# Second unit's state sums and half of its first outputs ahead of the first up-projections, in other banks

## The chip, the cores and the metric

The kernel runs on one core of one Trainium2 chip. The metric is the device time of one execution in microseconds (us), less is better; beside it stands the span of a profiled execution, from the first instruction of the program to the last. The engines are called as in the profile: PE (TensorE, matrix multiplications; PEld is its loading of weights), DVE (VectorE), ACT (ScalarE), POOL (GpSimd) and SP (SyncE, which issues most DMAs).

## The reference

A state-space scan in chunks over x (4 batches, 8 heads, 768 positions, 32 channels; states of 16), then a feed-forward block with a squared ReLU over the 3072 rows of 256 values that the scan gives:

```python
for c in range(nc):                        # chunks along the sequence
    cum = np.cumsum(log(a) of the chunk, axis=-1)
    L = np.exp(cum[:, :, :, None] - cum[:, :, None, :]) * causal
    M = np.einsum('bhin,bhjn->bhij', Cc, Bc) * L
    y_intra = np.einsum('bhij,bhjd->bhid', M, xc)
    y_inter = np.einsum('bhin,bhnd->bhid', Cc, state) * np.exp(cum)[..., None]
    y[:, :, sl] = y_intra + y_inter
    state = exp(sum of log(a)) * state + sum_j(decay_from_j * B_j x_j)
x = y.transpose(0, 2, 1, 3).reshape(B * S, H * D)
h = np.maximum(x @ w_in, 0.0)              # w_in: 256 x 2048
out = h * h @ w_out                        # w_out: 2048 x 256
```

## The kernel before

The work is cut into 12 units of 256 positions of one batch: units 0 to 3 are the first third of each batch, 4 to 7 the second, 8 to 11 the last. A unit is also a block of 256 rows of the feed-forward part, and the blocks are called a to l, so that unit 0 is block a and unit 1 is block b. Within a unit there are two halves of 128 positions with a state carried from one to the next.

For one of the first four units the steps are these, each a word of the list `ORDER` (lines 48 to 70), with the number of the unit behind it:

- `ldB`, `ldC`, `ldx` load B, C and x; `pb` and `pc` write B and the scaled C into `jt` (lines 169 to 188), `px` writes the scaled x into `xs` (line 190).
- `tr` turns `jt` round on PE (line 213), into two banks; `tc` copies that to `bct` in SBUF (DVE or ACT).
- `mt` computes the scores into the banks 0 to 3, 16 matmuls (line 243). `mk` is a mask multiplication on DVE straight out of a bank (line 252); `sc` copies a bank to SBUF on ACT (line 257), and `ms` masks that copy (line 261). Each `mk` or `sc` takes the next of the four banks, in the order 0, 1, 2, 3.
- `u` makes the state sums from `xs` and `jt`, 16 small matmuls (line 299); `us` copies them to SBUF (ACT, lines 349 and 352); `sf` makes from them the state `Sd` that the second half needs (DVE, line 396).
- `ina` and `inb` make the first outputs, each with two of the four masked score tiles and 16 matmuls (line 320); `ca` adds what the carried state gives (line 284).
- `t` copies the finished outputs into `T` (ACT or DVE, line 338), the input of the feed-forward part.

`p2` sums the second table of decays on PE (lines 529 to 642), and `pd` copies it to SBUF on ACT (lines 648 and 649). `id` are matmuls on constants whose result nobody reads (line 562).

The feed-forward part of a block has eight steps. Up-projection: `a0` is block a, step 0, four matmuls (line 475) into one bank, then a ReLU on ACT out of that bank (line 482); `qa0` squares it on DVE (line 488). Down-projection: `A0`, four matmuls (line 503), summed over the eight steps in bank 7 (bank 6 for block b). For the first four steps of block a the up-projection is in two parts: `al0` to `al3` make the two matmuls on the first half of the 256 inputs, `ah0` to `ah3` the two on the second half, and then the ReLU. The weights of `w_in` come in four DMAs that POOL issues, `wi0` to `wi3` (`wi0` and `wi1` hold the two halves of the inputs for the steps 0 to 3, `wi2` the steps 4 and 5, `wi3` the steps 6 and 7), those of `w_out` in `wo0` to `wo3`.

Every engine executes its own instructions in the order in which the list names them; between engines there are semaphores, set where one instruction writes what another reads, or writes over what another still reads. PSUM has eight banks of 512 columns. The list can name a bank (`al0@0`; `tr2@23` names two; `u1:57:6` puts the outputs of unit 1 into the banks 5 and 7 and the state sums of its first half into 6). Where it doesn't, a rotating list hands one out:

```python
turn = list(range(6))
def bank():
    h = want.pop(0) if want else next(h for h in turn if h not in busy)
    if h in turn:
        turn.remove(h)
        turn.append(h)
    return h
```

`busy` holds the banks that are taken in the order of the list: `mt` takes 0 to 3, and each `mk` or `sc` gives one back; `tr` takes two until its copies. A bank that an up-projection takes by itself is not held in `busy`; that its reader is done is seen to by the semaphores. For `u` without banks, the neighbouring free pair that stands earliest in `turn` is taken and moved to the end; the pair of `u3:45` is named and does not move anything in `turn`. At the word `bk`, in the third block, the list is set to 4, 5, 6.

Of the kernel before, what the change touches and what calls it, by code (L numbers as in the profile page):

```python
# [30 lines left out]
def kernel(  # L31
# [17 lines left out]
        fa1:a jz0:v ef jz1:p id3:512 ti fa0:s la0:s id4:512 pi eb ldB0:s ac0:v ldC0:a sk0 ku sp la1:a pbh0:p hd  # L49
        id1:256 pc0:v pbl0:v mb:a id1:384 trC0 ps iv:8:16 tcC0:1:a tcC0:0:v trB0 la2:s tcB0:2:v pk id1:512 iv1:0:8  # L50
        id1:512 ldx0:s mt0 hold wi0 la3:s px0:v ldC1:s su id2:512 ldB1:s wi1 ldx1:s u0:67 mk0 fq mk0 gC2:v mk0 ac1:v pc1:p sc0
        pb1:a jz2:a id2:512 tr1 id3:512 tc1:1:a tc1:0:v to ms0:p sf0 sk1 wo0 wi2 px1:p mt1 ina0 inb0 ca0 pp1:a mk1 mk1 t0:aa
        sc1 us0 mk1 fr p2@4 pd al0@0 al1@1 ldC2:s al2@5 al3@7 u1::6 ina1 ms1:v wo1 wi3 pc2 inb1 sf1 ca1 t1:va ah0 us1 ah1 qa0 ah2
        ldB2:s qa1 ah3 wo2 b0@2 qa2 qa3 qb0 b1@3 qb1 b2@4 b3@5 A0 A1 pb2:p tr2 B0 B1 zb0 qb3 gB3:v ldx2:s ldB3:s ldC3:s ldx3:s b4 a4
        iv:32:64 zb1 tc2:1:v tc2:0:v b5 sb1 sb0 qb4 a5 qb2 qa4 mt2 sc2 B3 iv:16:32 px2 pc3 wo3 px3 mk2 mk2 sc2 A3
        A2 ms2:v ms2:v qa5 a6 b6 pb3:a B2 a7 qb5 b7 u2 ina2 inb2 sf2 ld4 A4 tr3 ca2 tc3:1:v t2:aa B4 us2 B5
        tc3:0:v qa6 u3:45 pc4 mt3 A5 us3 sc3 c5 qb7 qb6 mk3 za3 pb4 ldC5:s ldB5:s c3 qa7 c4 qc5 c0 qc3 px4 tr4 ldx5:s pb5
        pc5 sa3 c1 c6 ldC6:s tr5 ldB6:s ldx6:s qc4 qc0 A6 px5 pq A7 wm c2 B6 c7 C0 ms3:v mk3 qc6 mk3 qc7 afC2 pc6 B7
# [838 lines left out]
```

## Time and profile before

| | |
|---|---|
| time, median of 3 runs | 114.05 us (113.71 to 114.88) |
| the profiled execution: time | 114.34 us |
| the profiled execution: span | 112.6 us |
| PE busy | 107.0 us (95%) |
| DVE, ACT, POOL busy | 82.2 us (73%), 76.9 us (68%), 49.5 us (44%) |
| granted TensorE clock | 1.000 |

A line of the timeline gives the start and the duration in us, the engine, the line of the kernel, the operation, what is written and read, how many instructions are drawn together, and in brackets the idle time of the engine before it and what ended that. The ends of matmuls are modelled, so that the matmuls of one group overlap those of the next by up to some 0.2 us. A line of the table of stretches gives for each engine the busy time and the number of instructions, and then the granted clock, the DMA share and the rate.

### The profile page before, as it was taken

The page shows a single profiled execution, that of the slowest core. Times are in us where ns is not written, and L with a number is a line of the kernel's source. Part 1 is how long each engine was busy: PE and PEld are TensorE (multiplying, and loading weights), DVE is VectorE, ACT ScalarE, POOL GpSimd, SP SyncE. Part 2 cuts the span into 40 slices and gives each one's busy share as a digit, 9 for nine tenths or more (in the row PEclk, how much of TensorE's full clock was granted, in tenths as well). Part 3 has the DMA queues.
Part 4 walks back from the last instruction along what each step waited for, and adds up shares of the span by engine and source line. Part 5 has one row for each costly group of instructions (what it writes and reads, how often), then busy time and mean ns, then how long its engine had stood idle before and what let it go on. Part 6 is the DMA issues. An engine that isn't in the chain of part 4 may idle for free.

```text
span 112.6 us, 3683 instructions
## 1 busy us (share of the span) xinstructions
PE 107.0 (95%) x1451; PEld 92.1 (82%) x1452; DVE 82.2 (73%) x190; ACT 76.9 (68%) x159; POOL 49.5 (44%) x96
## 2 busy tenths in 40 slices
PE   6988699999999999999999999999999999999990
PEld 2435589897998989989979989889899899899980
DVE  1689558996993898979966999779489298355440
ACT  1557487976894785685687686777876867866840
POOL 7579651488476574286074883283340020000000
PEclk9999999999999999999999999999999999999999
DMA  1999999499889899997897867799940020020203
GB/s 35 200 188 175 206 204 221 82 206 183 127 173 116 101 278 69 101 183 85 108 168 107 188 99 75 161 135 108 182 122 0 6 96 0 23 76 0 93 0 93
DMA packets 67025, 13.44 MB, mean 119 GB/s; under 512 B 63104, under 2 KB 65472, under 8 KB 67008
## 3 DMA queue, kind: packets, MB, share of 16 engines
q1 hardware_dynamic: 64320, 10.88, 63.2%
q0 software_dynamic: 1408, 2.10, 10.8%
q10 hardware_dynamic: 1280, 0.23, 1.1%
q8 instruction: 11, 0.18, 0.7%
q14 instruction: 6, 0.05, 0.2%
HBM read 10.58 MB, written 3.15 MB: 122 GB/s over the span
## 4 chain that ended last, share of the span: by engine, by line
PE 88%; DMA 3%; SPq 3%; ACT 2%; issue 1%; DVE 0%; ACTq 0%
PE pp L459 76%; PE pp L268 7%; DMA B_nat<-in_B_dram 3%; PE pp L237 2%; PE pp L243 2%; SPq L664 1%; SPq L138 1%; PE pp L213 1%; PE pp L562 1%; ACT T L226 1%; ACT sc L257 0%; DVE Sd L396 0%; ACT jt L183 0%; SPq L121 0%; ACT osl L855 0%
## 5 line engine op out<-in xcount | busy, mean ns | idle before, releaser
L482 ACT ACTIVATE hb<-pp 128x512 bf16<-128x512 f32 x96 | 54.5, 605 | 21.0 <-PE pp L459 19.5
L459 PE MATMUL pp<-T,w_in_b 128*128 128x256 bf16 x384 | 53.5, 273 | 0.8 <-ACT P_sb L649 0.8
L459 PE MATMUL pp<-w_out_b,h 128*128 128x256 bf16 (+1 forms) x400 | 53.9, 268 | 0.0
L488 DVE TENSOR_TENSOR h<-hb 128x512 bf16<-128x512 bf16 x96 | 44.0, 474 | 13.0 <-ACT hb L482 12.3
L459 PEld LDWEIGHTS <-w_in_b 128*128 128x128 bf16 x384 | 41.4, 114 | 2.9 <-issue 1.1
L459 PEld LDWEIGHTS <-h 128*128 128x128 bf16 x400 | 37.6, 98 | 4.5 <-issue 1.0
L252 DVE TENSOR_TENSOR mts<-pp,mask 128x512 bf16<-128x512 f32 x43 | 28.5, 677 | 0.8 <-PE pp L237 0.8
L195 POOL TENSOR_TENSOR xs<-x_nat,Pinv 128x256 bf16<-128x256 f32 (+1 forms) x19 | 14.0, 750 | 11.7 <-DMA x_nat<-in_x_dram 8.7
L384 POOL TENSOR_TENSOR Sd<-z,Pquad 128x256 bf16<-128x256 f32 x16 | 10.7, 679 | 12.3 <-DVE z L368 7.3
L175 POOL TENSOR_TENSOR jt<-C_nat,P_sb 128x128 bf16<-128x128 f32 x22 | 9.7, 460 | 9.1 <-DMA C_nat<-in_C_dram 7.3
L368 DVE SCALAR_TENSOR_TENSOR z<-z,Ptot,us 128x64 f32<-128x64 f32 x8 | 3.0, 372 | 6.8 <-ACT us L352 4.8
L562 PE MATMUL pp<-const-bfloat16-1.0 128*128 128x512 bf16 (+2 forms) x17 | 6.3, 491 | 1.0 <-PEq L881 0.8
L183 POOL CAST jt<-B_nat 128x256 bf16<-128x256 f32 x9 | 4.3, 476 | 6.6 <-DMA B_nat<-in_B_dram 4.5
L510 ACT COPY osb<-pp 128x512 f32<-128x512 f32 x11 | 6.4, 583 | 0.4 <-PE pp L459 0.4
L268 PE MATMUL pp<-mts,xs 64*32 64x128 bf16 (+1 forms) x288 | 5.4, 219 | 0.0
L268 PE MATMUL pp<-bct,Sd 128*128 128x128 bf16 x40 | 4.2, 220 | 0.2 <-DVE Sd L396 0.2
L268 PEld LDWEIGHTS <-xs 64*32 64x32 bf16 (+1 forms) x288 | 3.6, 93 | 0.4 <-issue 0.2
L562 PEld LDWEIGHTS <-const-bfloat16-1.0 128*128 128x128 bf16 x18 | 1.6, 114 | 2.5 <-issue 2.2
L268 PEld LDWEIGHTS <-Sd 128*128 128x128 bf16 x40 | 3.0, 98 | 0.7 <-DVE Sd L396 0.4
L226 ACT CAST T<-pp 128x256 bf16<-128x256 f32 x5 | 1.8, 373 | 2.6 <-PE pp L268 2.4
L268 PEld LDWEIGHTS <-jt 64*32 64x32 bf16 (+1 forms) x128 | 1.6, 90 | 1.9 <-issue 0.8
L257 ACT CAST sc<-pp 128x512 bf16<-128x512 f32 x5 | 2.9, 608 | 0.3 <-PE pp L243 0.2
(80 smaller groups left out, 59.5 us busy)
## 6 DMA issues: line engine op xcount, KB each, us to landing
out_dram<-osb SPq DMA_DIRECT2D x11, 256.0 KB, 2.9
x_nat<-in_x_dram SPq DMA_DIRECT2D x6, 256.0 KB, 4.4
w_in_b<-in_moe_w_in_dram POOLq DMA_DIRECT2D x4, 256.0 KB, 7.2
w_out_b<-in_moe_w_out_dram POOLq DMA_DIRECT2D x4, 256.0 KB, 6.7
B_nat<-in_B_dram SPq DMA_DIRECT2D x6, 128.0 KB, 4.0
C_nat<-in_C_dram SPq DMA_DIRECT2D x12, 64.0 KB, 3.5
B_nat<-in_B_dram SPq DMA_DIRECT2D x12, 64.0 KB, 3.5
x_nat<-in_x_dram SPq DMA_DIRECT2D x6, 128.0 KB, 3.2
```

The lines of the kernel that those rows point to most:

```text
L175: eng.tensor_tensor(out=_fap(jt[k % 3], 128 + 144 * g, [[384, 2], [32, 4], [1, 16]]), in0=_fap(loaded[k]["C"], 128 * g, [[16, 2], [32, 4], ...
L183: fn(out=_fap(jt[k % 3], 0, [[384, 2], [16, 2], [32, 4], [1, 16]]), in_=_fap(loaded[k]["B"], 0, [[16, 2], [128, 2], [32, 4], [1, 16]]))
L195: eng.tensor_tensor(out=_fap(xs, 256 * r, [[256, 2 // n], [32, 8], [1, 32]]), in0=_fap(loaded[k]["x"], 32 * r, [[32, 2 // n], [64, 8], [1, ...
L252: nc.vector.tensor_tensor(out=live[k]["mts"][:, q].rearrange("p r g i -> p (r g i)"), in0=pp[:, q, :], in1=mask1 if k >= LATE else mask, o ...
L268: nc.tensor.matmul(dst, w, v, start=bool(need), stop=False, skip_group_check=True, **({} if pos is None else {"tile_position": pos}))
L368: nc.vector.scalar_tensor_tensor(out=z, in0=prev[0], scalar=Ptot[:, total(1, b, j - 1):total(1, b, j - 1) + 1], in1=us, op0=ALU.mult, op1= ...
L384: nc.gpsimd.tensor_tensor(out=_fap(S_d, 0, [[128, 2], [32, 4], [1, 32]]), in0=_fap(z, 0, [[32, 2], [0, 4], [1, 32]]), in1=_fap(Pquad, 4 * ...
L459: nc.tensor.matmul(dst, w(0, 128), v, skip_group_check=True, **flags)
L482: nc.scalar.activation(out=hb.rearrange("p i t -> p (i t)"), in_=pp[:, h, :], func=AF.Relu)
L488: nc.vector.tensor_tensor(out=h2, in0=hb, in1=hb, op=ALU.mult)
L510: nc.scalar.copy(out=osb, in_=pp[:, 6 if blk == 1 else 7, :])
L562: nc.tensor.matmul(pp[:, h, 0:int(cols)], ones_b[:, 0:128], ones_b[:, 0:int(cols)] if dep is None else dep, start=True, stop=True, skip_gr ...
```

## The change

It changes only the list of the order, in four of its lines.

```diff
@@ -49,10 +49,10 @@
-        pb1:a jz2:a id2:512 tr1 id3:512 tc1:1:a tc1:0:v to ms0:p sf0 sk1 wo0 wi2 px1:p mt1 ina0 inb0 ca0 pp1:a mk1 mk1 t0:aa
-        sc1 us0 mk1 fr p2@4 pd al0@0 al1@1 ldC2:s al2@5 al3@7 u1::6 ina1 ms1:v wo1 wi3 pc2 inb1 sf1 ca1 t1:va ah0 us1 ah1 qa0 ah2
-        ldB2:s qa1 ah3 wo2 b0@2 qa2 qa3 qb0 b1@3 qb1 b2@4 b3@5 A0 A1 pb2:p tr2 B0 B1 zb0 qb3 gB3:v ldx2:s ldB3:s ldC3:s ldx3:s b4 a4
-        iv:32:64 zb1 tc2:1:v tc2:0:v b5 sb1 sb0 qb4 a5 qb2 qa4 mt2 sc2 B3 iv:16:32 px2 pc3 wo3 px3 mk2 mk2 sc2 A3
+        pb1:a jz2:a id2:512 tr1 id1:512 tc1:1:a tc1:0:v to ms0:p sf0 sk1 wo0 px1:p wi2 ina0 inb0 mt1 ca0 pp1:a mk1 mk1 t0:aa
+        us0 sc1 mk1 fr p2@4 u1:57:6 ina1 pd al0@0 al1@1 ldC2:s al2@2 al3@3 ms1:v wo1 wi3 pc2 inb1 sf1 ca1 t1:va ah0 us1 ah1 qa0 ah2
+        ldB2:s qa1 ah3 wo2 b0@4 qa2 qa3 qb0 b1@0 qb1 b2@1 b3@5 A0 A1 pb2:p tr2@23 B0 B1 zb0 qb3 gB3:v ldx2:s ldB3:s ldC3:s ldx3:s b4@0 a4@1
+        iv:32:64 zb1 tc2:1:v tc2:0:v b5@4 sb1 sb0 qb4 a5@5 qb2 qa4 mt2 sc2 B3 iv:16:32 px2 pc3 wo3 px3 mk2 mk2 sc2 A3
```

In words:

- Two of the three idle matmuls behind `tr1` go. `ina0 inb0` come before `mt1` on PE.
- On POOL the scaling of x for unit 1 (`px1`) comes before the issue of the DMA `wi2`, which stood ahead of it.
- On ACT the copy of unit 0's state sums (`us0`) comes before a score copy of unit 1 (`sc1`).
- `u1` and `ina1`, 32 matmuls, move on PE from behind the eight matmuls of `al0` to `al3` to ahead of them. The outputs of unit 1 go to the banks 5 and 7; the rotating list had given 2 and 3. The sums of its first half stay in bank 6; those of its second lie in bank 7, where the list had given 3.
- `al2` and `al3` use the banks 2 and 3, where it was 5 and 7; `b0` to `b3` the banks 4, 0, 1, 5 where it was 2, 3, 4, 5. `tr2`, `b4`, `a4`, `b5` and `a5`, which had taken their banks from the rotating list (0 and 1, 2, 3, 4, 5), now name 2 and 3, 0, 1, 4, 5.

The words that follow (among them `mk2 mk2 sc2 A3 A2 ... a6 b6 ... a7 ... b7 u2 ... tr3 ... u3:45 ... mt3 ... sc3 c5 qb7 qb6 mk3 ... c3`) are the same; those without a named bank go on taking theirs from `turn` as these words leave it.

## The prediction

> **What bounds the kernel now.** I read the page first, then the busy time in stretches, then the timeline of the opening, where the edits are.
>
> ```profile
> span 112.6 us, 3683 instructions
> ...
> PE 88%; DMA 3%; SPq 3%; ACT 2%; issue 1%; DVE 0%; ACTq 0%
> ```
>
> The chain that ended last is PE's for 88% of the span. The table of stretches says where PE is not full (us, then per engine the busy time and the number of instructions, then granted clock, DMA share, GB/s):
>
> ```profile
> core 0: us, PE busy (x) PEld busy (x) DVE busy (x) ACT busy (x) POOL busy (x), PEclk, DMA share, GB/s
> 9.30:12.40 3.10, 2.27 (x71) 1.27 (x68) 3.10 (x8) 2.49 (x10) 3.08 (x6) 1.00 1.16 177
> 12.40:14.40 2.00, 1.76 (x59) 1.39 (x60) 0.80 (x3) 0.00 (x0) 0.62 (x2) 1.00 1.18 209
> 14.40:19.10 4.70, 4.70 (x47) 4.32 (x46) 2.94 (x8) 4.50 (x11) 1.95 (x4) 1.00 1.20 217
> 19.20:23.60 4.40, 4.40 (x55) 3.88 (x53) 4.40 (x13) 3.18 (x7) 2.40 (x3) 1.00 0.68 119
> 23.60:28.00 4.40, 4.40 (x115) 3.56 (x112) 3.38 (x10) 3.37 (x9) 3.79 (x8) 1.00 1.14 195
> 28.00:97.00 69.00, 69.00 (x926) 62.33 (x914) 56.30 (x124) 49.86 (x100) 31.00 (x55) 1.00 0.80 114
> ```
>
> Up to 14.40 PE has holes: 0.83 us in the first stretch shown, 0.24 in the second. From 14.40 to 97 it has none. So whatever lets PE begin its unbroken run earlier shows in full at the end, unless something later isn't ready for it; and every new wait of PE after 14.40 costs its full length, as there is no hole to make it good. In 19.20 to 23.60 DVE has no hole either: there the two engines run side by side with nothing to spare.
>
> **The opening.** The timeline around the moved work:
>
> ```profile
> 5.69 1.26 POOL L154 DMA_DIRECT2D w_in_b<-in_moe_w_in_dram x2
> ...
> 9.15 0.81 PE L562 MATMUL pp<-const-bfloat16-1.0 128*128 128x512 bf16 x3
> ...
> 9.91 0.42 PE L243 MATMUL pp<-bct 32*64 32x256 bf16 x16
> ...
> 9.97 0.71 POOL L156 DMA_DIRECT2D w_in_b<-in_moe_w_in_dram x1
> ...
> 10.70 1.06 POOL L195 TENSOR_TENSOR xs<-x_nat,Pinv 128x512 bf16<-128x512 f32 x1
> ...
> 11.37 0.61 ACT L257 CAST sc<-pp 128x512 bf16<-128x512 f32 x1
> 11.70 0.59 POOL L160 DMA_DIRECT2D w_out_b<-in_moe_w_out_dram x1
> 11.85 0.30 ACT L349 COPY us<-pp 128x128 f32<-128x128 f32 x1
> ...
> 12.18 0.41 DVE L261 TENSOR_TENSOR mts<-sc,mask 128x512 bf16<-128x512 bf16 x1
> ...
> 12.39 0.80 PEld L459 LDWEIGHTS <-w_in_b 128*128 128x128 bf16 x8 [0.92 <-DMA w_in_b<-in_moe_w_in_dram]
> 12.40 1.06 PE L459 MATMUL pp<-T,w_in_b 128*128 128x256 bf16 x8 [0.83 <-ACT P_sb L649]
> 13.39 0.25 PE L268 MATMUL pp<-xs,jt 64*32 64x64 bf16 x16
> ...
> 13.46 0.57 PE L268 MATMUL pp<-mts,xs 64*32 64x128 bf16 x32
> 13.79 0.42 DVE L396 TENSOR_TENSOR Sd<-pp,Pquad 128x256 bf16<-128x256 f32 x1 [1.20 <-PE pp L268]
> ...
> 14.27 0.29 PE L268 MATMUL pp<-bct,Sd 128*128 128x128 bf16 x2 [0.24 <-DVE Sd L396]
> ...
> 14.39 1.84 PE L459 MATMUL pp<-T,w_in_b 128*128 128x256 bf16 x15
> 14.60 0.37 ACT L226 CAST T<-pp 128x256 bf16<-128x256 f32 x1 [2.21 <-PE pp L268]
> ...
> 15.55 3.58 ACT L482 ACTIVATE hb<-pp 128x512 bf16<-128x512 f32 x7
> ```
>
> The first up-projections (`al`, 12.40) begin with the landing of their weights at 12.39. The `P_sb` copy that the next line names ends in the same instant, but `al` neither reads it nor writes its bank; I take the DMA. Two idle matmuls fewer and `ina0 inb0` before `mt1` therefore move nothing that counts: `mt1` still waits for its transposed input, the idle matmuls were cover, and ACT, which copies out the first outputs and then `us`, is behind anyway. I cost these at nothing; the 0.83 us hole covers them.
>
> Into that hole, 11.57 to 12.40, now go `u1` (0.25) and half of the 32 first outputs (half of 0.57): 0.54 together. They need `xs` and, because their banks 6 and 7 hold unit 0's sums, the copy `us`. With `us0` in the place of the score copy, at 11.37, it ends at 11.67 instead of 12.15; the score copy comes 0.3 later, still before DVE is free for its mask at 12.18. `al2` and `al3` now need the banks that this copy and DVE's third mask empty, both done by 12.3. `xs` starts between 9.98 (`wo0` issued, if x has landed) and 10.70, and ends by 11.76. So the 0.54 lie between 11.76 and 12.30 at the latest: free, with 0.1 to spare.
>
> After `al`, at 13.39, only `inb1` and `ca1` remain. In the trace 1.00 us lie between 13.39 and the first `ah` at 14.39: the 48 small matmuls, the wait for `Sd`, and 0.12 from `ca1` to `ah`. `Sd` can now be made on DVE right behind the mask of 12.18, by 12.59 + 0.42 = 13.01, so its wait is gone; 16 matmuls take 0.2 to 0.29, `ca1` its 0.12. That leaves 0.32 to 0.41, a gain of **0.6 to 0.68**. Next in line is the second half of the weights for `ah`: issued at about 6.32, and by the 7.2 us that are the median for this tile it lands at 13.5, in time.
>
> ```profile
> DMA to landing us min/median/max: 6.7/7.2/8.2
> ```
>
> By the longest, 8.2, it would be 14.5 and the gain nothing; that end is kept for a rival. `wi2` is issued behind `xs`, up to 1.8 us later, at about where `wo1` is issued now (11.70), and `wo1` and `wi3` some 0.7 later. `b4`, which reads it, stands at 19.30 and would stand at 18.7; 11.7 + 6.7 to 7.2 is 18.4 to 18.9. I take 0 and keep 0.2 for the range. The other rows that bound the gain:
>
> ```profile
> 16.72 0.67 POOL L183 CAST jt<-B_nat 128x256 bf16<-128x256 f32 x1 [1.04 <-DMA B_nat<-in_B_dram]
> ...
> 17.98 0.43 PEld L213 LDWEIGHTS <-jt 128*128 128x128 bf16 x6
> ```
>
> `tr2` reads what POOL finishes at 17.39, held by a DMA that doesn't move, and loads at 17.98: it can come 0.59 earlier and no more. Against that, the waits of `b1` and `b3` for banks (they waited for `us1` and for the ReLU of `a2`) mostly go, as `b3`'s new bank is free early. I carry on with **0.6**. ACT's seven ReLUs back to back (to 19.13) begin with the copy at 14.60 and shift with it, and so does DVE, which follows them.
>
> **The banks later on.** This part decides. After `a5` the rotating list reads 0 1 2 3 4 5 before; with the new names it reads 2 3 0 1 4 5. The next words without a bank thus change: `a6 b6 a7 b7` had 0 1 2 3 and get 2 3 0 1. All four are given out behind `mt2`, whose scores fill 0 to 3, and these are emptied in the order `sc2` (bank 0, ACT), `mk2` (1, DVE), `mk2` (2, DVE), `sc2` (3, ACT). `a6` now wants the bank that DVE empties second.
>
> ```profile
> 22.41 1.22 DVE L252 TENSOR_TENSOR mts<-pp,mask 128x512 bf16<-128x512 f32 x2
> ...
> 22.82 1.04 PE L459 MATMUL pp<-T,w_in_b 128*128 128x256 bf16 x8
> ```
>
> The two masks end at 23.63; `a6` stands at 22.82 and needed only the bank of `sc2`. DVE is full from 19.20 to 23.60, so the masks come earlier by no more than the 0.6 by which its first ReLU does: 23.03. `a6` starts there at the earliest, say 23.06: **0.24 later than now, the 0.6 spent** and PE idle for 0.84. `b6`'s bank is freed by ACT earlier, `a7` and `b7` are behind.
>
> The same again one unit on. `tr3` had 0 and 1 and gets 2 and 3, so the list stands at 0 1 4 5 2 3 instead of 2 3 4 5 0 1 when `c5` and `c3` ask, while `mt3` fills 0 to 3. They had 4 and 5, free long before; now `c5` gets 0, just given back by `sc3`, and `c3` gets 1, just given back by `mk3`.
>
> ```profile
> 27.45 1.72 DVE L488 TENSOR_TENSOR h<-hb 128x512 bf16<-128x512 bf16 x3
> ...
> 28.27 1.37 POOL L195 TENSOR_TENSOR xs<-x_nat,Pinv 128x256 bf16<-128x256 f32 x2 [0.51 <-PE pp L243]
> ...
> 28.52 2.78 PE L459 MATMUL pp<-T,w_in_b 128*128 128x256 bf16 x24
> 29.09 0.68 DVE L252 TENSOR_TENSOR mts<-pp,mask 128x512 bf16<-128x512 f32 x1
> ```
>
> In the 2.78 us row `c5` starts at 28.52 and `c3` four matmuls later, (2.78 - 0.2) / 6 = 0.43, at 28.95. The mask `mk3` ends at 29.77, and with 0.03 for the semaphore `c3` starts at 29.80: **0.84 lost** (the wait of `c5` for its own bank lies inside). The mask follows `tr3` on PE through DVE's copies and three squares, so it shifts with PE and this wait stays. After `bk` both lists are the same.
>
> The three squares take 1.72 us, where three of the mean that the page gives would take 1.42:
>
> ```profile
> L488 DVE TENSOR_TENSOR h<-hb 128x512 bf16<-128x512 bf16 x96 | 44.0, 474 | 13.0 <-ACT hb L482 12.3
> ```
>
> POOL's `xs` runs beside them. If the overlap falls otherwise, `c3`'s wait is 0.54 instead of 0.84. The Trainium skill, "SBUF — State Buffer", section "Who interferes with whom", says of such a pair that whichever issues first holds the shared port for its whole instruction and the other blocks; by that the 0.3 us would fall on POOL if the squares came first, and the sum would be 0.3 lower.
>
> **The sum**: -0.6 + 0.84 + 0.84 = +1.08 us. The profiled execution would go from 114.34 to 115.4 (span 113.7). It stood 0.29 above the median, so the median goes from 114.05 to **115.1**.
>
> **Rivals.**
>
> - *The bank waits don't bind.* The masks are early enough, or the first 0.84 is made up elsewhere, and the 0.6 stays: 113.45. For it: the trace of before has hardly a bank wait. Against: DVE is at 4.40 of 4.40. Chance 0.10.
> - *One of the two waits binds*, the other is halved or more: -0.6 + 0.84 = +0.24, so 114.3. Chance 0.12.
> - *The opening gives nothing, the waits stay.* `u1` now stands ahead of `al` in PE's queue, and behind `u1` everything: if x or `xs` is late, past 11.86, `al` waits for it, and if the second weights land by the 8.2, `ah` stays at 14.4. Then the masks stay at 23.63, `a6` starts at 23.66: 0.84 + 0.84, 115.7, slower by 1.5%. For it: x has no row of its own landing. Against: POOL took `xs` at 10.70 without a wait. Chance 0.18.
> - *The clock drops.* PE gets idle stretches of 0.8 us in place of idle matmuls; if the clock were halved over the 2.78 us behind the second, that is 2.8 more: 117.9. The granted clock was 1.00 in every row, with 0.83 idle at 11.57. Chance 0.03. The Trainium skill, "TensorE: Matmul & The Clock Gate", section "A second HAM failure mode: psum-queue depth-cycling", tells of such oscillation from short idle times between groups, with a window of some 3.4 us; half speed for one window would be 1.7, so 116.8 by the page. No stretch here shows it.
>
> **The numbers.** The forecast has the remaining 0.57; its own range is 114.8 to 115.6 (the squares' 0.3 below, 0.2 for `wi2` and 0.3 of a smaller gain above). The range 114.1 to 116.0 leaves out the first rival, the last, and a tail. About 1% is what a measurement tells from no change: 112.91 to 115.19 is "same". Of the forecast some 0.33 lies below 115.19 and 0.24 above; with rival one (0.08) and two (0.12) "same" has 0.53 or so, "faster" the edge of rival one, 0.02, and "slower" 0.45 with rivals three and four.
>
> **What would show it.** In the profile after: `u1` and 16 first outputs on PE before 12.40; the first `ah` near 13.75 instead of 14.39; then an idle time of PE of about 0.8 us before `a6`, ended by a DVE mask (line 252), near 23.0; then one before `c5` and a longer one before `c3`, about 0.8 together, ended by line 257 and line 252; and nothing new after. I am wrong if PE has no hole after 14, if `a6` starts before 22.8, or if `al` starts after 12.5.

## The result, and the profile after

| | before | after |
|---|---|---|
| median | 113.82 us (113.57 to 114.88, 6 runs) | 115.3 us (115.19 to 115.59, 6 runs) |
| the profiled execution: time, span | 114.34, 112.6 us | 115.19, 113.5 us |

The ratio after to before is 1.0121, 95% interval 1.0081 to 1.0162. The forecast was 115.1. Some of the runs further down come out more than 1.5% above the fastest of their kernel; the ratios, and the medians of the experiments, leave these out.

The chain that ended last, on the page after, where PE had 88% and DVE next to nothing:

```profile
PE 79%; DVE 6%; ACT 3%; DMA 3%; SPq 3%; issue 2%; ACTq 0%
```

The table of stretches after (columns as before):

```profile
9.30:12.50 3.20, 2.38 (x99) 1.62 (x98) 2.62 (x7) 2.39 (x10) 3.18 (x6) 1.00 1.12 175
12.50:13.96 1.46, 1.46 (x33) 1.15 (x27) 0.91 (x4) 0.00 (x0) 0.76 (x3) 1.00 1.20 215
13.96:19.10 5.14, 5.14 (x52) 4.93 (x51) 3.69 (x11) 4.47 (x10) 1.34 (x4) 1.00 1.16 194
19.20:23.20 4.00, 3.19 (x42) 2.52 (x41) 4.00 (x11) 3.03 (x6) 2.19 (x3) 1.00 0.83 146
23.20:28.00 4.80, 4.80 (x104) 4.13 (x103) 3.25 (x9) 3.36 (x8) 3.96 (x8) 1.00 1.20 199
28.00:97.00 69.00, 68.86 (x927) 61.83 (x923) 56.13 (x123) 49.47 (x98) 31.48 (x55) 1.00 0.72 113
```

PE's holes have moved from the opening into the stretch from 19.20 to 23.20, where DVE is full (4.00 of 4.00), and one more lies behind 28. First two rows of PE before, then PE's timeline after, from the first `ah` on, then DVE's and a row of ACT's:

```profile
21.50 1.49 PE L459 MATMUL pp<-w_out_b,h 128*128 128x256 bf16 x12
...
28.07 0.61 PE L459 MATMUL pp<-w_out_b,h 128*128 128x256 bf16 x4
```

```profile
13.96 2.82 PE L459 MATMUL pp<-T,w_in_b 128*128 128x256 bf16 x24
...
20.89 1.48 PE L459 MATMUL pp<-w_out_b,h 128*128 128x256 bf16 x12
23.19 1.03 PE L459 MATMUL pp<-T,w_in_b 128*128 128x256 bf16 x8 [0.81 <-DVE mts L252]
...
28.08 0.42 PE L243 MATMUL pp<-bct 32*64 32x256 bf16 x16
28.44 0.61 PE L459 MATMUL pp<-w_out_b,h 128*128 128x256 bf16 x4
29.19 2.94 PE L459 MATMUL pp<-T,w_in_b 128*128 128x256 bf16 x24
```

```profile
21.92 1.22 DVE L252 TENSOR_TENSOR mts<-pp,mask 128x512 bf16<-128x512 f32 x2
...
27.63 1.50 DVE L488 TENSOR_TENSOR h<-hb 128x512 bf16<-128x512 bf16 x3
29.06 0.68 DVE L252 TENSOR_TENSOR mts<-pp,mask 128x512 bf16<-128x512 f32 x1
```

```profile
28.55 0.58 ACT L257 CAST sc<-pp 128x512 bf16<-128x512 f32 x1
```

`ah` starts at 13.96 instead of 14.39. The down-projections ahead of `a6` start at 20.89 instead of 21.50 in the profile before, 0.6 early, and then `a6` waits until the second mask has ended (21.92 + 1.22 = 23.14): 23.19 instead of 22.82. Matmuls of this kind start 0.109 us apart, and the last of the twelve starts at 22.11, so without the wait `a6` would have stood at 22.22; the wait is 0.97. The row shows 0.81 of it as idle time, as the end of the last matmul is modelled later. The row names DVE's line 252 as what ended it. Behind the scores at 28.08, `c5` starts 0.75 after the down-projection at 28.44, where it was 0.45 in the profile before: 0.3 lost to ACT's copy of its bank, which ends at 29.13. The 24 matmuls from 29.19 take 2.94 us where they took 2.78: 0.16 more in front of `c3`, which starts at 29.79, just behind the end of the mask at 29.74. Neither shows as idle time in a row.

### The profile page after: what moved, and what is told of

The parts are those of the page before. It is cut to its first block, busy times and chain, and to the rows that moved or that the text cites. A ratio compares the mean times of both kernels' runs of the same rounds, so it can differ in the third digit from the quotient of the medians.

```text
span 113.5 us, 3674 instructions
## 1 busy us (share of the span) xinstructions
PE 107.2 (95%) x1449; PEld 92.0 (81%) x1450; DVE 82.6 (73%) x190; ACT 77.0 (68%) x158; POOL 49.7 (44%) x96
## 4 chain that ended last, share of the span: by engine, by line
PE 79%; DVE 6%; ACT 3%; DMA 3%; SPq 3%; issue 2%; ACTq 0%
PE pp L459 69%; PE pp L268 7%; DMA B_nat<-in_B_dram 3%; ACT hb L482 2%; DVE mts L252 2%; PE pp L237 2%; DVE h L488 2%; SPq L664 1%; PE pp L243 1%; SPq L138 1%; DVE bct L228 1%; PE pp L213 1%; ACT sc L257 1%; DVE T L228 0%; ACT jt L183 0%
## 5 line engine op out<-in xcount | busy, mean ns | idle before, releaser
L368 DVE SCALAR_TENSOR_TENSOR z<-z,Ptot,us 128x64 f32<-128x64 f32 x8 | 2.5, 317 | 6.3 <-ACT us L352 5.0
L562 PE MATMUL pp<-const-bfloat16-1.0 128*128 128x512 bf16 (+2 forms) x15 | 5.7, 499 | 1.0 <-PEq L881 0.8
L268 PE MATMUL pp<-mts,xs 64*32 64x128 bf16 (+1 forms) x288 | 5.9, 219 | 0.8 <-DVE Sd L396 0.6
L183 POOL CAST jt<-B_nat 128x256 bf16<-128x256 f32 x9 | 3.8, 418 | 3.9 <-DMA B_nat<-in_B_dram 3.9
L335 ACT CAST T<-pp 128x512 bf16<-128x512 f32 x3 | 1.8, 586 | 1.7 <-PE pp L268 1.7
```

Source lines behind the costliest of these rows:

```text
L183: fn(out=_fap(jt[k % 3], 0, [[384, 2], [16, 2], [32, 4], [1, 16]]), in_=_fap(loaded[k]["B"], 0, [[16, 2], [128, 2], [32, 4], [1, 16]]))
L268: nc.tensor.matmul(dst, w, v, start=bool(need), stop=False, skip_group_check=True, **({} if pos is None else {"tile_position": pos}))
L562: nc.tensor.matmul(pp[:, h, 0:int(cols)], ones_b[:, 0:128], ones_b[:, 0:int(cols)] if dep is None else dep, start=True, stop=True, skip_gr ...
```

## The experiments

**The banks alone, and the change without them.** In `e1_banks_back` the change keeps its opening and the later words name the banks they had before:

```diff
-        ... qa5 a6 b6 pb3:a B2 a7 qb5 b7 u2 ... A4 tr3 ca2 ... sc3 c5 ... c3 qa7 c4 qc5 c0 ... c1 c6 ... c2 B6 c7
+        ... qa5 a6@0 b6@1 pb3:a B2 a7@2 qb5 b7@3 u2 ... A4 tr3@01 ca2 ... sc3 c5@4 ... c3@5 qa7 c4@0 qc5 c0@1 ... c1@4 c6@5 ... c2@0 B6 c7@1
```

> The change as it is, with the later banks named as they were before (a6 b6 a7 b7 in 0 1 2 3, tr3 in 0 1, c5 c3 c4 c0 c1 c6 c2 c7 in 4 5 0 1 4 5 0 1). Theory (the waits for banks at a6 and at c5, c3 are the loss; 0.97 and 0.47 us in the profile after): PE has no hole behind 14.4, and the time is 115.3 - 1.44 = 113.9 us, within 0.3 of before; lower, to 113.3, if the opening keeps its 0.6. Rival (the new opening itself, or the DMA order in it, costs the time): it stays near 115.3.

`e2_only_banks` is the opposite: the kernel before with only the banks that the change's list hands out.

```diff
-        ... qa5 a6 b6 pb3:a B2 a7 qb5 b7 u2 ... A4 tr3 ca2 ... sc3 c5 ... c3 qa7 c4 qc5 c0 ... c1 c6 ... c2 B6 c7
+        ... qa5 a6@2 b6@3 pb3:a B2 a7@0 qb5 b7@1 u2 ... A4 tr3@23 ca2 ... sc3 c5@0 ... c3@1 qa7 c4@4 qc5 c0@5 ... c1@0 c6@1 ... c2@4 B6 c7@5
```

> The kernel before, its opening untouched, with only the later banks as the change hands them out (a6 b6 a7 b7 in 2 3 0 1, tr3 in 2 3, c5 c3 c4 c0 c1 c6 c2 c7 in 0 1 4 5 0 1 4 5). Theory: a6 starts when the second mask has ended, at 23.67 instead of 22.82 (0.85 lost), c3 0.47 to 0.84 later by its mask: 113.8 + 1.3 to 1.7 = 115.1 to 115.5 us. Rival (the opening is what costs): 113.8, no change.

| | ratio to before | 95% interval | median |
|---|---|---|---|
| the change | 1.0121 | 1.0081 to 1.0162 | 115.3 us |
| `e1_banks_back` | 1.0032 | 1.0004 to 1.0061 | 114.03 us |
| `e2_only_banks` | 1.0134 | 1.0094 to 1.0173 | 115.2 us |

(The kernel before was at 113.77 beside the last two.) The banks alone cost what the whole change costs, and without them the change is within 0.6% of before. PE at `a6` in the two:

```profile
22.26 1.04 PE L459 MATMUL pp<-T,w_in_b 128*128 128x256 bf16 x8
```

```profile
22.93 1.03 PE L459 MATMUL pp<-T,w_in_b 128*128 128x256 bf16 x8 [0.70 <-DVE mts L252]
```

The first is `e1_banks_back`, with no wait; the second is `e2_only_banks`, where the masks end at 21.66 + 1.22 = 22.88. So the loss is the banks'. At the second place `e2_only_banks` differs from the change: only `c5` waits.

```profile
28.18 0.61 PE L459 MATMUL pp<-w_out_b,h 128*128 128x256 bf16 x4
28.93 2.78 PE L459 MATMUL pp<-T,w_in_b 128*128 128x256 bf16 x24
```

```profile
27.53 1.09 DVE L488 TENSOR_TENSOR h<-hb 128x512 bf16<-128x512 bf16 x3
28.54 0.69 DVE L252 TENSOR_TENSOR mts<-pp,mask 128x512 bf16<-128x512 f32 x1
```

Between the down-projection and `c5` lie 0.75 again, 0.3 too much, but the 24 matmuls take 2.78, so `c3` does not wait: the mask has ended at 29.23.

The opening, which was to bring 0.6, brings nothing: `e1_banks_back` is 0.3% above before, not 0.5% below.

**One of the two places at a time.** `e3_first_back` names only `a6@0 b6@1 a7@2 b7@3` as before, and keeps the others of the change; `e4_second_back` names only `tr3` and block c's as before.

> The change with a6 b6 a7 b7 back in 0 1 2 3, the later ones as the change has them. Theory: the wait of 0.97 before a6 goes, that before c5 and c3 stays, at 0.47 to 0.84: 115.3 - 0.97 = 114.3 us, up to 114.7. Rival (one wait only moves the other, as DVE's masks set the pace of both): 115.0 or more.

> The change with tr3 and the up-projections of block c back in their banks, a6 to b7 as the change has them. Theory: the wait before a6 stays, those before c5 and c3 go: 115.3 - 0.47 = 114.8 us, 114.5 if their price is 0.84 as the prediction had it. Rival (those two waits cost nothing at the end): 115.3.

`e3_first_back`: 1.0091 (1.0054 to 1.0128), median 114.4; `e4_second_back`: 1.0109 (1.0078 to 1.0141), median 114.9. Taking `e1_banks_back` off, the second place alone costs 0.0059 x 113.8 = 0.7 us and the first 0.0077 x 113.8 = 0.9 us; the two together, in the change, 0.0089 x 113.8 = 1.0. With intervals some 0.8 us wide it cannot be said from the times whether one wait takes some of the other. Each costs something without the other, so the rival that only one binds is out. Against the change itself, measured on another occasion, putting one place back gains no more than 0.3 us (the first) or 0.1 us (the second), inside the intervals; what one wait costs beside the other stays open. In the profile of `e3_first_back` the second place costs 0.3 at `c5` and 0.22 at `c3`.

The profile of `e4_second_back` has an accident that bears on what sets `a6`. There PE stood still before `tr2`, as B of unit 2 landed late (PE, then POOL):

```profile
18.98 0.51 PE L213 MATMUL pp<-eye_b,jt 128*128 128x128 bf16 x6 [1.38 <-POOL jt L183]
```

```profile
18.54 0.39 POOL L183 CAST jt<-B_nat 128x256 bf16<-128x256 f32 x1 [3.36 <-DMA B_nat<-in_B_dram]
```

and then the wait before `a6` was only 0.3 (24.02, where the twelve matmuls from 22.40 end their turn at 23.71): most of the time that PE lost ahead of the wait is not lost again at it, as the masks were late by less (they end at 23.96, 0.82 later than in the profile after) than PE (1.51).

**The opening.** What failed is seen in the profile after, in PE's and DVE's timeline:

```profile
9.97 0.47 PE L268 MATMUL pp<-mts,xs 64*32 64x128 bf16 x32 [0.56 <-DVE Sd L396]
10.36 0.42 PE L243 MATMUL pp<-bct 32*64 32x256 bf16 x16
...
11.63 0.25 PE L268 MATMUL pp<-xs,jt 64*32 64x64 bf16 x16
11.70 0.22 PE L268 MATMUL pp<-mts,xs 64*32 64x128 bf16 x1
12.18 0.40 PE L268 MATMUL pp<-mts,xs 64*32 64x128 bf16 x15 [0.26 <-DVE mts L252]
12.51 1.06 PE L459 MATMUL pp<-T,w_in_b 128*128 128x256 bf16 x8
```

```profile
9.50 0.41 DVE L396 TENSOR_TENSOR Sd<-pp,Pquad 128x256 bf16<-128x256 f32 x1
...
10.83 1.89 DVE L252 TENSOR_TENSOR mts<-pp,mask 128x512 bf16<-128x512 f32 x3 [0.58 <-PE pp L243]
```

The first outputs write the banks 6 and 7, and DVE is still reading unit 0's state sums out of other columns of bank 6 for `Sd`, until 9.91. Put ahead of the scores, they hold those back: 10.36 instead of 9.91, with 0.56 us of PE idle ahead. DVE's masks of unit 1 begin at 10.83 instead of 10.38, `ina1` waits for the second mask, and `al`, now behind `ina1`, starts at 12.51, although here its weights had landed at 10.20. Two edits test this: `e5_scores_first` is `e1_banks_back` with `mt1` back ahead, and `e6_only_outputs_first` the kernel before with that one edit.

```diff
@@ e5_scores_first, against e1_banks_back
-        ... px1:p wi2 ina0 inb0 mt1 ca0 ...
+        ... px1:p wi2 mt1 ina0 inb0 ca0 ...
@@ e6_only_outputs_first, against before
-        ... px1:p mt1 ina0 inb0 ca0 ...
+        ... px1:p ina0 inb0 mt1 ca0 ...
```

> The change with the later banks back, and the scores of unit 1 (mt1) ahead of unit 0's first outputs (ina0 inb0) again; all else as the change has it. In the profiles with the new order the first outputs wait for the state Sd (DVE line 396, until 9.92), as they write the banks from which it is made, and the scores behind them begin at 10.36 instead of 9.9. Theory (this wait is what the opening costs): scores, masks, al and the first ah come 0.3 to 0.45 us earlier, ah near 13.5; the time is 0.3 to 0.45 below that of the change with the banks back, 113.8 us, level with before or up to 0.3 below it. Rival (the landing of the second weights sets ah in any case): no change from the change with the banks back, 114.2.

> The kernel before with one edit: ina0 inb0 ahead of mt1. Theory: mt1 begins 0.45 us later, the masks of unit 1 end 0.45 later, al1 to al3, which write banks that these masks empty or stand behind one that does, come later, and the first ah by 0.3 to 0.45: 113.8 + 0.3 to 0.45 = 114.1 to 114.25 us. Rival (0.8 us of PE idle there hides it, as the prediction had it): 113.8, no change.

`e5_scores_first`: 0.9987 (0.9953 to 1.0022), median 113.77; `e6_only_outputs_first`: 1.0024 (0.9988 to 1.006), median 114.09, beside 113.97 of before. The intervals of the times don't separate either from no change. The profiles do; the scores, the first `al` and the first `ah` start at (us):

| | order | scores | `al` | `ah` |
|---|---|---|---|---|
| before | scores first | 9.91 | 12.40, by the weights | 14.39 |
| `e2_only_banks` | opening of before | 9.74 | 11.64, by the weights | 13.64 |
| `e6_only_outputs_first` | of before, outputs first | 10.45 | 11.84 | 14.02 |
| after | outputs first | 10.36 | 12.51 | 13.96 |
| `e1_banks_back` | outputs first | 10.41 | 12.55 | 14.00 |
| `e5_scores_first` | of the change, scores first | 9.75 | 11.95 | 13.40 |

Two things stand in it. In the change's opening the order of the scores is worth 0.6 us of `ah` (14.00 against 13.40, in neither of which the weights set `al`). In the opening of before it is worth less: `ah` is 0.38 later in `e6_only_outputs_first` than in `e2_only_banks`, and 0.2 of that is the later landing of its weights. And the same opening of before reached `ah` at 14.39 in one execution and at 13.64 in another, since the weights of `al` landed 0.75 earlier in the second:

```profile
11.64 1.06 PE L459 MATMUL pp<-T,w_in_b 128*128 128x256 bf16 x8 [0.24 <-DMA w_in_b<-in_moe_w_in_dram]
```

The prediction was measured against an execution in which they were late; against the other, the change's opening is 0.3 slower, which is what `e1_banks_back` shows in the times. The 12.35 us at which these weights landed in the profile before are the latest of fourteen profiles: 10.96 to 12.35 in the eight that issue `wi2` ahead of `px1`, 10.20 to 11.81 in the six that issue it behind. Whether the later issue of `wi2` brings the first weights in earlier, which would be a gain of the change, no run here isolates.

**What a better version meets.** `e7_half_after` is `e5_scores_first` with `ina1` behind `al`; `e8_weights_first` has `wi2` ahead of `px1` on POOL again.

```diff
@@ e7_half_after, against e5_scores_first
-        ... u1:57:6 ina1 pd al0@0 al1@1 ldC2:s al2@2 al3@3 ms1:v ...
+        ... u1:57:6 pd al0@0 al1@1 ldC2:s al2@2 al3@3 ina1 ms1:v ...
@@ e8_weights_first, against e5_scores_first
-        ... wo0 px1:p wi2 ...
+        ... wo0 wi2 px1:p ...
```

> As e5_scores_first, with ina1 (half of unit 1's first outputs) behind al again, and only u1 ahead of it. If the weights of al land after 12, the 16 matmuls lie in PE's idle time in e5 and no longer here: 0.2 us slower than e5. If they land before 11.6, PE is full either way, and the two are equal within 0.1 us.

> As e5_scores_first, with the DMA wi2 issued ahead of px1 on POOL again, as before. xs then ends near 11.65 instead of 10.93, and u1, and behind it ina1 and al, begin 0.1 to 0.25 us later than in e5: up to 0.25 us slower where the weights have landed, no change where they land after 12. Rival (the early weights are worth more than the early xs, b4 waits): faster than e5.

`e7_half_after`: 0.9958 (0.9911 to 1.0005), median 113.64; `e8_weights_first`: 0.9952 (0.9905 to 1.0000), median 113.56. They are the best found and lie level with each other and, within the intervals, with `e5_scores_first`. That they beat the kernel before is not settled: the intervals reach no change, and the best of several variants tends to look better than it is. In `e8_weights_first` `u1` waits 0.23 for `xs`, as expected, and `ah` starts at 13.57, 0.17 later than in `e5_scores_first`; that doesn't show in the time, because `e5_scores_first` loses its lead again: `c5` starts at 27.69 in it and at 27.68 in `e8_weights_first`, and `A6` at 30.58 and 30.30. PE of `e5_scores_first` at `A6`:

```profile
27.69 2.78 PE L459 MATMUL pp<-T,w_in_b 128*128 128x256 bf16 x24
30.58 1.03 PE L459 MATMUL pp<-w_out_b,h 128*128 128x256 bf16 x8
```

24 matmuls take 2.62 of PE's turn (0.109 each), so `A6` could start at 30.31 and starts at 30.58. That wait ends with the landing, at 30.54, of the fourth load of `w_out`, which `A6` reads and which POOL had issued at 24.89 behind `px2` and `pc3`. Two moves were made against the loads: `tr2` behind `B0 B1` (in `e9_turn_behind`), and that load, `wo3`, ahead of `px2 pc3` on POOL (in `e10_wo3_early`), each on `e8_weights_first`; both together in `e11_both`, and both on the kernel before in `e12_before_both`.

```diff
@@ e9_turn_behind, against e8_weights_first
-        ... A0 A1 pb2:p tr2@23 B0 B1 zb0 ...
+        ... A0 A1 pb2:p B0 B1 tr2@23 zb0 ...
@@ e10_wo3_early, against e8_weights_first
-        ... iv:16:32 px2 pc3 wo3 px3 ...
+        ... iv:16:32 wo3 px2 pc3 px3 ...
```

> As e8_weights_first, with tr2 behind B0 and B1 on PE. tr2 needs B of unit 2, whose landing differs much between executions (13.8 to 18.5 us in the profiles so far), and where it is late PE stands still ahead of tr2 (1.5 us in the profile of e4_second_back, 0.9 in that of e6_only_outputs_first). Theory (this is what spreads the times, and a bound of the opening's gain): the median falls by 0.1 to 0.4 us from e8, and fewer runs lie a microsecond above the lowest. Rival (the late landing is caught up elsewhere, or the copies behind tr2 are late next): no change.

> As e8_weights_first, with the DMA wo3 issued ahead of px2 and pc3 on POOL. In e5_scores_first PE waited 0.27 us at A6 (30.58) for these weights, 0.1 in e1_banks_back, so that part of the opening's gain ends there. Theory: no wait at A6, up to 0.3 us off where the opening is early; 0.1 in the median. Rival (256 KB more in the queues while x of unit 2 and C, x of unit 3 are loading): px2, pc3 or u3 come later, 0 to 1 us slower.

> Both moves, tr2 behind B0 and B1 and wo3 early, on e8_weights_first: if each takes away its own wait, 113.2 us, 0.5 to 0.7 below before. If the loads are the bound, e8 or worse.

> The kernel before with the same two moves, its opening and its banks untouched. If the two moves alone make the difference, it is as good as e11_both; if the opening of the change (u1 and ina1 ahead of al, banks put right, scores first) is worth something of its own, it lies 0.2 to 0.4 us above it.

Ratios, in this order: 1.0014 (0.9976 to 1.0052), 1.005 (1.0002 to 1.0098), 1.0039 (0.9999 to 1.008) and 1.0018 (0.9972 to 1.0064). None is better than the kernel before, and the early load is, if anything, worse; `e8_weights_first` was not run again beside them, and `e12_before_both` does not come out above `e11_both`, so this pair shows no gain of the opening either. In the three profiles with the early load x of unit 3 lands at 26.5 to 27.3 us, in the ten others that show its landing at 24.8 to 25.5. In `e12_before_both` PE waits for the `xs` that is made from it:

```profile
28.20 0.25 PE L268 MATMUL pp<-xs,jt 64*32 64x64 bf16 x16 [0.67 <-POOL xs L195]
```

(The profile of `e10_wo3_early` also lost 1.77 us ahead of `tr2`, where B of unit 2 was late; that lies before the moved load is issued, at 20.43, and is no cost of the move.) So, in these profiles, the gain of an earlier opening ends at loads whose landings it does not move. Which of them ends it differs from execution to execution, and how much of the gain of `e8_weights_first` is real stays open.

## Why the prediction was right

- *What bounds the kernel*: held. PE's unbroken run decides, and its new waits show in full: the profile lost 0.97 and 0.47 at them, gained 0.6 ahead of the first, +0.84 us by sum, and its span went up by 0.9.
- *The banks later on*: the mechanism was right at both places and in both sequences; `e1_banks_back` and `e2_only_banks` show that it accounts for the loss. The sizes: 0.97 for the forecast 0.84 at `a6`, as the masks came 0.49 earlier than before and not 0.6; 0.47 for 0.84 at `c5` and `c3`, and there the longer wait is that of `c5`, not of `c3`. The second is the term that the prediction said could be 0.54. PE was 0.37 later at this place than in the profile before, but DVE's mask no later at all (29.06 for 29.09), so that the wait did not shift with PE: from the copies behind `tr3` to the mask DVE took 1.97 us instead of 2.37, the two copies 0.62 instead of 0.81 and the three squares 1.50 instead of 1.72. Of the squares' part 0.17 fell on the first: in the profile before it ran beside POOL's copy of B (until 27.76) and took 0.59, in the profile after it began at 27.63, when that copy had ended at 27.50, and took 0.42. The third ran beside `xs` both times and took 0.87 and 0.84. In `e2_only_banks` each of the three took 0.42, and POOL's first `xs` 0.91 where it took 0.62 in the profile before: there the cost fell on POOL, and `c3` did not wait. The Trainium skill's rule that was named there ("SBUF — State Buffer", "Who interferes with whom") the traces bear out in part: of a square and the `xs` beside it the one gets slower, or both do (0.84 and 0.83 in the profile after).
- *The opening*: the step that failed is that `ina0 inb0` ahead of `mt1` "move nothing that counts". It delayed the scores by 0.45, as the first outputs write a bank that is still being read. `al` therefore started at 12.51 with its weights long there, just past the 12.5 that the prediction named as a sign of being wrong, and 0.46 us lay between its last matmul's turn and `ah` where 0.32 to 0.41 were forecast: `ah` came 0.43 earlier and not 0.6. The 0.6 was found at `tr2` in the profile (17.49 for 18.09), but only against an execution of before whose weights came late. In the times the opening costs 0.3%, and with the scores first again it is level or a little better. That the median rose by 1.48, where the profiled executions differ by 0.85, fits that: of the six runs of before, four lie at 113.57 to 113.84, below the profiled one's 114.34.
- *The number* was partly luck. The forecast difference was +1.08 and the measured one +1.48; that 115.1 lies so near 115.3 is because three more runs took the median of before from 114.05 to 113.82. Two errors also worked against each other: the opening's gain was put too high and the second wait too high.
- *`wi2` and the second weights* in time: held. In the profile after the second weights landed at 12.57, ahead of `ah`, and `wi2` at 16.26, 2.4 us ahead of `b4`.
- *The rivals*: that the opening gives nothing (0.18) was nearer the measured difference, with 0.84 + 0.84 = 1.68, than the forecast. What took the gain was not what this rival named (x, or the second weights) but the first outputs ahead of the scores. Its own condition did occur elsewhere: x of unit 1 landed at 9.31 in the profile after, but at 11.33 in that of `e11_both`, where `u1` waited for `xs` until 12.57 and `al` started at 12.97. The clock stayed at 1.00 in every stretch with 0.81 us idle before `a6`; what the Trainium skill tells of short idle times between groups ("TensorE: Matmul & The Clock Gate") is shown by no run here.

## What to carry to other kernels

Where buffers are handed out by a rotation, a change to one step changes the buffers of every later step that takes its own from it: replay the rotation over the whole list and ask of each step that got another buffer who empties that one, and when. In this kernel a write into a PSUM bank waits for whoever still reads any column of that bank (0.56 us in the profile after), so an operation moved ahead can hold up its queue even if its inputs are ready. And before a gain is counted against a wait in one profile, look whether the wait is there in other executions: a landing that differs by 0.75 us between two executions of the same opening made and unmade the whole gain here.

## What was not expected of the hardware

The landing of one DMA, issued at nearly the same time in all these kernels, differed widely between executions. The load of B of unit 2 was issued between 8.86 and 9.11 us in all fourteen profiles and landed between 13.84 and 18.48. POOL's conversion of it began at 14.88 in the profile after, at 16.72 in the one before and at 18.54 in that of `e4_second_back`, and in the last PE stood still for it. How much of the spread of the times comes from that is not shown: `e9_turn_behind`, which moves its reader on PE back, came out level with the kernel before (1.0014) and was not run beside `e8_weights_first`, on which it is built.
